# First states on ScalarE's queue, the first half of x in two parts, 23 constant products ahead, and another instruction list: an attention and two-expert-layer kernel on one core

## The chip, the cores and the metric

One core of a Trainium2 chip runs the whole program in one launch. The metric is the device time of one execution in microseconds, lower is better; of several executions the median counts. TensorE (PE) multiplies matrices into PSUM, VectorE (DVE) and ScalarE (ACT) work on tiles in SBUF and PSUM, SyncE (SP) issues transfers. Each engine takes its instructions strictly in the order in which they stand in its own list, and engines wait for each other by semaphores.

## The reference, cut to what matters

```
def _attn_ref(x, state):              # x 4x8x512x64, state 4x8x32x64
    scores = scale * x @ state^T      # softmax over the 32 states -> a
    xread = a @ state
    scores2 = scale * state @ x^T     # softmax over the 512 rows of x -> a2
    sread = a2 @ x
    return concat([xread, sread], axis=2)
def _moe_ref(x, w_in, w_out):         # 2176 tokens, 512 -> 2048 -> 512
    h = x @ w_in
    return (h * tanh(softplus(h))) @ w_out
def _moe2_ref(x, w_gate, w_val, w_out, rms_g):   # 512 -> 1536 -> 512
    xn = x / rms * rms_g
    g = xn @ w_gate
    return (silu(g) * (xn @ w_val)) @ w_out
```

The attention output of four batches (b = 0 to 3) feeds the first layer, and that one feeds the second.

## The kernel before

The kernel records some 2400 operations (`op`), each with its engine, what it reads and writes and a function that issues its instructions. `Plan.run` then goes through a table of numbers, `SEQ`, and issues the operations in exactly that sequence; a number's half is the operation, and an odd number puts an operation that either ScalarE or VectorE can do on VectorE. So `SEQ` alone sets the order in which the instructions stand on each engine and, for the copies that both can do, the engine.

Operands are split into a high and a low float16 part, which costs VectorE and ScalarE much preparation. The first two of four blocks of the first layer for batch 0 (`full_group`) skip the split and use float32 products, so that TensorE has work while the weights are prepared.

What stands at the start, and is touched here:

- `rouse` (L1681) issues 28 products of a constant tile `ones` into an accumulator before anything is loaded. `stir` (L762) issues 40 further products of constants, spread between the first operations of batch 0.
- `load_state` (L631) fetches the states. A batch's 32 states of 8 heads come in two halves, r = 0 and r = 1 (even and odd heads), 32 KB each, on SyncE's queue. For batch 0 a copy of the first half (L393, "COPY attm<-attm") is put behind the second half, so that two transposes give both pairings of heads.
- `attention(0)` (L671) fetches x of batch 0 in two halves of 512 KB (L691), one for even and one for odd heads. TensorE transposes each half in two pieces (L723, four transposes each, into a PSUM bank), which ScalarE or VectorE copies to SBUF (tile `tt`). TensorE transposes the states (L699), VectorE copies them (L393, "COPY attm<-p"), and then the scores of the first half are formed (L754, 16 small products in four accumulators' quarters).
- Of the scores, "s1" is the softmax over states (transposition L793, maxima L807, subtraction L808, exponential L810 on ScalarE, sums and reciprocals L814 to L816, product L819, transposition back L821) and "s2" the one over rows of x (maxima L799 to L802, exponentials L805 on ScalarE).
- Between them VectorE and ScalarE turn the first weights into float32 (L395 and L391 "w<-psm", L501, L508, L512, joined at L528).
- The first real product of the first layer (L999, `l1`) needs the transposed softmax of L821 and the folded weights of L972. Its results go through ScalarE (L1009) to the second product (L1023).
- ScalarE loads a table of functions at the start (L1701), before its first copy.

Of the kernel before, what the change touches and what calls it, by code (L numbers as in the profile page):

```python
# [232 lines left out]
def attn_moe_moe_kernel(  # L233
# [359 lines left out]
    def seven(w, u, m, at, pool, after, store):  # L593
# [33 lines left out]
        for j, n in ((0, 512), (512, 1024), (1536, 1024), (2560, 1024)):  # L627
            split(m, at + j, at + 256 + j + (512 if j else 0), n, s, ((w, u), "s"), f"{w}{u}{j // 512 + 2 if j else 0}")


    def load_state():  # L631
        sv = state.rearrange("b (k r) n d -> b r k n d", r=2)
        for b in range(B):
            for r in range(2):
# [1165 lines left out]
```

## Time and profile before

| what | value |
|---|---|
| runs of the kernel before | 700.97, 701.10, 701.89 us, median 701.1 |
| profiled execution | 702.01 us |
| its span in the trace | 700.2 us |
| TensorE busy | 691.1 us (99%) |
| VectorE busy | 645.3 us (92%) |
| ScalarE busy | 423.1 us (60%) |
| transfers | 101.04 MB, mean 144 GB/s |

The span runs from the first instruction's start to the last one's end; the profiled execution's own time is 1.8 us longer and 0.9 us above the median. In the timeline a row holds the start, the time until the group ends, the engine ("PEld" is TensorE's weight load, "SPq" an issue of a transfer by SyncE), the line, the operation, output and input tiles, shapes, the number of instructions, and in brackets how long the engine had idled and what ended that. Matmuls overlap one another, so a group's pace is read from starts.

### The profile page before, as it was taken

Reading aid. Unit: us, or ns where it says so; the run is one execution under the profiler, and the core shown is the slowest. Engines: PE = TensorE matmul, PEld = TensorE weight load, DVE = VectorE, ACT = ScalarE, POOL = GpSimd, SP = SyncE. Lnnn points to the kernel's source line nnn. Section 1 sums busy time; section 2 is a strip of 40 time slices with the busy share of each in tenths; the row PEclk is TensorE's granted clock in tenths of the full one; section 3 lists DMA queues with packets and bytes.
Section 4 is the critical chain, followed back from the end, with each engine's and each line's share of the span. In section 5 each row is a group of like instructions: output and inputs, shape, how many; then the busy total and the mean of one; then the engine's idle time right before and its main releaser. Section 6 shows DMA issues by size and latency. Waiting matters only on the chain.

```text
span 700.2 us, 14144 instructions
## 1 busy us (share of the span) xinstructions
PE 691.1 (99%) x5834; PEld 491.8 (70%) x5834; DVE 645.3 (92%) x1135; ACT 423.1 (60%) x689; POOL 0.7 (0%) x6
## 2 busy tenths in 40 slices
PE   8999999999999999999999999999999999999997
PEld 6645444444444444476988889988889988899886
DVE  5999999999999999999999998989898897888997
ACT  5999999998877789999947465312212212121330
POOL 0000000000000000000000000000000000000000
PEclk9999999999999999999999999999999999999999
DMA  6977523255255463465800012620455432330233
GB/s 220 284 245 228 182 66 116 65 192 161 81 209 212 168 224 121 150 242 193 334 1 31 31 61 85 232 93 16 136 212 196 152 121 106 135 107 31 91 107 135
DMA packets 42611, 101.04 MB, mean 144 GB/s; under 512 B 16692, under 2 KB 18740, under 8 KB 40116
## 3 DMA queue, kind: packets, MB, share of 16 engines
q1 hardware_dynamic: 42548, 100.15, 41.7%
q8 instruction: 45, 0.74, 0.4%
q14 instruction: 18, 0.15, 0.1%
HBM read 67.90 MB, written 32.24 MB: 143 GB/s over the span
## 4 chain that ended last, share of the span: by engine, by line
PE 56%; DVE 9%; DMA 1%; ACT 1%; issue 1%; SPq 0%; DVEq 0%
PE p L1276 31%; PE a L1360 15%; PE a L1141 4%; PE p L1505 2%; PE p L1073 2%; DMA kept_wg<-attm 1%; DVE g L1103 1%; PE a L1549 1%; DVE attm L625 1%; DVE psm L625 1%; DVE rms L1182 1%; DVE attm L560 1%; DVE rms L955 1%; DVE attm L528 1%; DVE attm L395 1%
## 5 line engine op out<-in xcount | busy, mean ns | idle before, releaser
L1141 PE MATMUL a<-g,w2m 128*128 128x512 f16 (+1 forms) x864 | 162.7, 343 | 0.6 <-DVE slot L1158 0.6
L1141 PEld LDWEIGHTS <-w2m 128*128 128x128 f16 x864 | 75.8, 98 | 79.2 <-issue 4.4
L1276 PEld LDWEIGHTS <-attm 128*128 128x128 f16 x1008 | 98.3, 98 | 13.6 <-issue 2.1
L1276 PEld LDWEIGHTS <-w 128*128 128x128 f16 x1008 | 98.5, 98 | 11.3
L1288 DVE TENSOR_TENSOR tt<-p,tt 128x512 f32<-128x512 f32 x120 | 81.3, 686 | 17.9 <-PE p L1276 16.5
L1065 PE MATMUL p<-slot,rms 128*128 128x512 f16 x336 | 77.3, 379 | 0.3 <-ACT tt L1087 0.3
L1276 PE MATMUL p<-slot,w 128*128 128x256 f16 x576 | 69.3, 273 | 0.0
L1276 PE MATMUL p<-slot,attm 128*128 128x256 f16 x576 | 68.9, 273 | 0.0
L1360 PEld LDWEIGHTS <-w2m 128*128 128x128 f16 x576 | 56.4, 98 | 6.7 <-issue 0.2
L1065 PEld LDWEIGHTS <-rms 128*128 128x128 f16 x336 | 32.2, 98 | 40.9 <-issue 3.4
L1312 ACT ACTIVATE tt<-tt,page 128x512 f32<-128x512 f32 x36 | 25.2, 714 | 54.1 <-DVE tt L1288 54.1
L1360 PE MATMUL a<-attm,w2m 128*128 128x256 f16 x384 | 46.0, 273 | 0.0
L1360 PEld LDWEIGHTS <-g 128*128 128x128 f16 x432 | 42.3, 98 | 4.9
L391 ACT ACTIVATE w2m<-tt 128x512 f16<-128x512 f32 x30 | 18.4, 624 | 43.7 <-DVE tt L1338 21.7
L1087 ACT ACTIVATE tt<-p,page 128x512 f32<-128x512 f32 x60 | 40.3, 680 | 6.6 <-PE p L1065 4.1
L1103 DVE SCALAR_TENSOR_TENSOR g<-tt,page,g 128x1024 f16<-128x1024 f32 (+1 forms) x32 | 38.7, 1211 | 1.3 <-ACT g L391 1.2
L1319 DVE TENSOR_TENSOR w2m<-tt,w2m 128x512 f16<-128x512 f32 x51 | 34.6, 686 | 3.4 <-ACT w2m L391 3.1
L391 ACT ACTIVATE g<-tt 128x512 f16<-128x512 f32 x25 | 15.4, 624 | 36.4 <-DVE tt L1338 28.7
L391 ACT ACTIVATE tt<-p 128x512 f32<-128x512 f32 x31 | 17.9, 592 | 31.8 <-PE p L1276 17.5
L1360 PE MATMUL a<-attm,g 128*128 128x256 f16 x288 | 34.9, 273 | 0.0
L1338 DVE TENSOR_TENSOR tt<-tt 128x512 f32<-128x512 f32 x48 | 32.5, 686 | 0.5
L560 DVE SCALAR_TENSOR_TENSOR psm<-psm,page 128x1024 f16<-128x1024 f32 (+1 forms) x28 | 32.1, 1145 | 0.4 <-ACT psm L391 0.2
(243 smaller groups left out, 1227.4 us busy)
## 6 DMA issues: line engine op xcount, KB each, us to landing
psm<-in_moe_w_out_dram SPq DMA_DIRECT2D x14, 1024.0 KB, 6.3
psm<-in_moe_w_in_dram SPq DMA_DIRECT2D x8, 1024.0 KB, 7.3
psm<-part SPq DMA_DIRECT2D x7, 1024.0 KB, 6.8
psm<-in_moe_w_val_dram SPq DMA_DIRECT2D x6, 1024.0 KB, 5.3
part<-rms SPq DMA_DIRECT2D x24, 256.0 KB, 3.1
kept_wv<-psm SPq DMA_DIRECT2D x9, 512.0 KB
kept_w<-psm SPq DMA_DIRECT2D x9, 512.0 KB, 2.8
attm<-in_moe_w_gate_dram SPq DMA_DIRECT2D x4, 1024.0 KB, 6.2
```

Source lines behind the costliest of these rows:

```text
L391: nc.scalar.activation(o, i, ACTF.Copy, scale=1.0 if scale is None else scale)
L560: op({"V": v1(n) + 0.06}, lambda e: nc.vector.scalar_tensor_tensor(lo, f, s, h, ALU.mult, ALU.subtract), r=[*fn_, *hn, sname], w=ln, name= ...
L1065: nc.tensor.matmul(P[ph], P[folds[u][k]][:, a, f:f + 128], xh[:, k, b, :], start=(k, a, b) == (0, 0, 0), stop=(k, a, b) == (1, 1, 0))
L1087: op({"A": a_ps(512) + 0.1}, lambda e, sp=sp, i=i, ph=ph, ce=ce: nc.scalar.activation(P[sp][:, 512 * i:512 * i + 512], P[ph], ACTF.Mish, s ...
L1103: nc.vector.scalar_tensor_tensor(lo, x, rh, hi, ALU.mult, ALU.subtract)
L1141: nc.tensor.matmul(P[ya[d]][:, :n], part("wo", u, f, a)[:, d * 128:(d + 1) * 128], P[g[0]][:, g[1], b, i * n:(i + 1) * n], start=first and ...
L1276: nc.tensor.matmul(P[to][:, f * 256:f * 256 + 256], part(w, u, j, a)[:, k * 256 + f * 128:k * 256 + f * 128 + 128], h[:, k, b, :], start=b ...
L1288: op({"V": v1(512)}, lambda e: nc.vector.tensor_tensor(P[to], P[bank_], P[a], ALU.add), r=[bank_, a], w=[to], name=f"{w} add")
L1312: op({"A": a_ps(512) + 0.13}, lambda e, i=i, o=o: nc.scalar.activation(P[o], P[i], ACTF.Silu, scale=c3), r=[i, f"c3{u}"], w=[o], tab="silu ...
L1319: op({"V": v1(512)}, lambda e: nc.vector.tensor_tensor(P[g][:, 1, :], P[s], P[g][:, 0, :], ALU.subtract), r=[s], w=[g], name="gl")
L1338: op({"V": v1(512)}, lambda e: nc.vector.tensor_tensor(P[o], P[a], P[b], f), r=[a, b], w=[o], name="gsum")
L1360: nc.tensor.matmul(P[to][:, t * 256:t * 256 + 256], P[g][:, a, o:o + 128], part("w2", u, j, b)[:, f * 256:f * 256 + 256], start=begin and ...
```

## The change

The states of batch 0 are fetched by ScalarE's queue instead of SyncE's. ScalarE's load of the exponential table moves behind the issue of the second half. The first half of x of batch 0 is fetched in two transfers of 256 KB, the second half still in one. `rouse` issues 23 products, not 28. The bookkeeping that holds some buffers back ("hold") issues no instruction and is now one operation ahead of the loads. `SEQ` is replaced by another list of the same length less one entry for "hold" and plus one for the extra load, in which nearly every row differs.

```diff
 SEQ = [int(k) for k in """
-32 46 4 9 58 61 62 0 6 10 50 53 64 74 158 160 48 70 72 66 68 76 116 108 148 114 140 152 118 162 142 126 226 228 230
...
-    def load_state():
+    def load_state(hold):
         sv = state.rearrange("b (k r) n d -> b r k n d", r=2)
         for b in range(B):
             for r in range(2):
-                op({"D": 0.5}, lambda e, b=b, r=r: nc.sync.dma_start(out=sb[:, b, r, :], in_=sv[b, r]),
-                    w=[("state", b, r)], lat=1.9, name=f"state{b} load{r}")
+                def load(e, b=b, r=r):
+                    (nc.sync if b else nc.scalar).dma_start(out=sb[:, b, r, :], in_=sv[b, r])
+                    if (b, r) == (0, 1):
+                        nc.scalar.preload_act_table_set(TABLES["exp"])
+
+                op({"D": 0.5 if b else 0.2}, load, w=[("state", b, r), *([] if b else ["act queue"])], lat=1.9,
+                   after=[] if b else [hold], name=f"state{b} load{r}")
...
-            for r in range(2):
-                a_op({"D": 1.6}, lambda e, r=r: nc.sync.dma_start(
-                    out=P[xb][:, 2 * r:2 * r + 2, :].rearrange("p i (k n) -> p (i k) n", k=2), in_=xv[r]),
-                    r=xbl, w=[(xb, r, 0), (xb, r, 1)], lat=1.9, st=f"load r{r}")
+            for i, n_ in ((0, 1), (1, 1), (2, 2)):
+                k = 2 * i if i < 2 else 0
+                a_op({"D": 0.8 * n_}, lambda e, i=i, n_=n_, k=k: nc.sync.dma_start(
+                    out=P[xb][:, i:i + n_, :].rearrange("p i (k n) -> p (i k) n", k=2), in_=xv[i // 2][:, k:k + 2 * n_, :]),
+                    r=xbl, w=[(xb, i // 2, j) for j in (range(2) if n_ == 2 else [i])], lat=1.9, after=[hold], st=f"load r{i // 2}")
...
-        load_state()
+        load_state(hold)
         load_gain()
         op({"T": 4.0 * ROUSE / 38}, rouse, w=["warm"], name="rouse")
-        nc.scalar.preload_act_table_set(TABLES["exp"])
         state_scale()
-        attention(0)
+        attention(0, hold=hold)
...
-ROUSE, STIRS = 28, 40
+ROUSE, STIRS = 23, 40
```

ScalarE's list at the start of the program, before (p_84 to p_87 are PSUM banks with transposed x, a_88 and a_89 scores of the first half):

```order
L1701 ACT_TABLE_LOAD
L391 ACTIVATE tt<-p_85 128x512
L391 ACTIVATE tt<-p_87 128x512
L391 ACTIVATE tt<-p_84 128x512
L805 ACTIVATE attm,page_103<-a_88,page_69 128x256
```

and in the changed kernel (lines from L631 on are shifted by up to 6; L636 issues a half of the states, L638 loads the table):

```order
L636 DMA attm<-in_state_dram 128x1x64
L391 ACT_TABLE_LOAD
L391 ACTIVATE tt<-p_84 128x512
L636 DMA attm<-in_state_dram 128x1x64
L638 ACT_TABLE_LOAD
L391 ACTIVATE tt<-p_85 128x512
L391 ACTIVATE tt<-p_87 128x512
L391 ACTIVATE tt<-p_84 128x512
L811 ACTIVATE attm,page_102<-a_88,page_69 128x256
```

The first half of the states is ScalarE's first instruction; the second half stands behind ScalarE's first copy of transposed x, and a second table load stands between that and the next copy. VectorE had the first of these copies before.

SyncE's list at the start of the program, before:

```order
L691 DMA attm<-in_x_dram 128x4x256
L635 DMA attm<-in_state_dram 128x1x64 x2
L691 DMA attm<-in_x_dram 128x4x256
L479 DMA psm<-in_moe_w_in_dram 128x4x512 x2
L635 DMA attm<-in_state_dram 128x1x64 x2
```

and in the changed kernel:

```order
L697 DMA attm<-in_x_dram 128x2x256 x2
L697 DMA attm<-in_x_dram 128x4x256
L479 DMA psm<-in_moe_w_in_dram 128x4x512 x2
L636 DMA attm<-in_state_dram 128x1x64 x4
```

The second half of x and the first weights follow x's first half directly; the states of the later batches follow the weights, as before.

VectorE's list from its first copy to the second transposition of scores, before:

```order
L393 COPY attm<-attm 128x64
L393 COPY tt<-p_84 128x512
L393 COPY attm<-p_86 128x256
L793 STREAM_TRANSPOSE attm<-a_88 128x256
L793 STREAM_TRANSPOSE attm<-a_89 128x256
L799 TENSOR_REDUCE page_103<-a_88 128x1
L799 TENSOR_REDUCE page_103<-a_89 128x1
L801 TENSOR_REDUCE page_69<-page_103 128x1
L802 TENSOR_SCALAR page_69<-page_69 128x1
L807 TENSOR_REDUCE page_103<-attm 128x16
```

and in the changed kernel:

```order
L393 COPY attm<-attm 128x64
L393 COPY attm<-p_86 128x256
L805 TENSOR_REDUCE page_102<-a_88 128x1
L805 TENSOR_REDUCE page_102<-a_89 128x1
L807 TENSOR_REDUCE page_69<-page_102 128x1
L808 TENSOR_SCALAR page_69<-page_69 128x1
L799 STREAM_TRANSPOSE attm<-a_88 128x256
L799 STREAM_TRANSPOSE attm<-a_89 128x256
L813 TENSOR_REDUCE page_102<-attm 128x16
```

The maxima of the first half's scores now come ahead of their transposition; from here to the transposition back that the first real product waits for (L821, now L827) VectorE has the same 30 instructions in both kernels.

## Rows read from the trace of the kernel before

**Rows 1.** The page, part 1: busy us, share of the span, instructions

```profile
PE 691.1 (99%) x5834; PEld 491.8 (70%) x5834; DVE 645.3 (92%) x1135; ACT 423.1 (60%) x689; POOL 0.7 (0%) x6
```

**Rows 2.** TensorE's waits, whole span: us in total, times, longest us

```profile
PE a L1141 <- DVE slot L1158: 0.6, 1, 0.6
PE p L1276 <- DVE tt L1288: 0.6, 1, 0.6
...
PE p L1187 <- DVE rms L1182: 0.4, 1, 0.4
...
PE a L1023 <- DVE w2m L528: 0.3, 1, 0.3
PE p L1065 <- ACT tt L1087: 0.3, 1, 0.3
```

**Rows 3.** Stretches: length, busy of PE, PEld, DVE, ACT, POOL, clock, DMA

```profile
50.00:75.00 25.00, 25.00 (x104) 12.16 (x103) 23.98 (x57) 24.77 (x37) 0.00 (x0) 1.00 0.74 237
75.00:100.00 25.00, 25.00 (x194) 11.57 (x192) 24.32 (x46) 24.82 (x39) 0.00 (x0) 1.00 0.41 128
```

**Rows 4.** Timeline, 0 to 22 us

```profile
0.73 1.28 ACT L1701 ACT_TABLE_LOAD   x1 [0.73 <-PEq L1785]
...
0.73 0.44 SPq L691 DMA_DIRECT2D attm<-in_x_dram  x1
...
1.05 5.17 PE L1686 MATMUL a<-ones 128*128 128x256 f16 x28 [1.05 <-DVE ones L1691]
...
1.23 1.36 SPq L635 DMA_DIRECT2D attm<-in_state_dram  x2
...
4.78 0.20 DVE L393 COPY attm<-attm 128x64 f32<-128x64 f32 x1 [3.64 <-DMA attm<-in_state_dram]
...
6.06 1.04 PE L723 MATMUL p<-ident,attm 128*128 128x128 f32 x8
6.69 0.69 DVE L393 COPY tt<-p 128x512 f32<-128x512 f32 x1 [1.71 <-PE p L723]
...
6.82 0.25 PEld L699 LDWEIGHTS p<-ident,attm 128*128 128x128 f32 x2
...
7.13 0.60 ACT L391 ACTIVATE tt<-p 128x512 f32<-128x512 f32 x1 [5.12 <-PE p L723]
...
7.83 0.67 PE L754 MATMUL a<-tt,attm 64*32 64x256 f32 x16 [0.52 <-DVE attm L393]
...
8.58 0.78 DVE L793 STREAM_TRANSPOSE attm<-a 128x256 f32<-128x256 f32 x2 [0.81 <-PE a L754]
...
21.20 0.65 DVE L821 STREAM_TRANSPOSE tt<-attm 128x512 f32<-128x512 f32 x1
...
21.91 0.70 PE L999 MATMUL p<-tt,rms 128*128 128x512 f32 x1 [0.36 <-DVE tt L821]
```

**Rows 5.** TensorE's timeline, two pieces of the constant products

```profile
1.05 4.02 PE L1686 MATMUL a<-ones 128*128 128x256 f16 x18 [1.05 <-DVE ones L1691]
...
4.87 1.24 PE L1686 MATMUL a<-ones 128*128 128x256 f16 x9
```

**Rows 6.** Line L723 within 0 to 10 us: TensorE's own wait for x

```profile
L723 PEldq EVENT_SEMAPHORE  x1: 51/51/51, 4.5 to 4.5; - x1
```

**Rows 7.** The stretch from the first scores on VectorE to L821, columns as rows 3

```profile
8.58:21.20 12.62, 11.45 (x155) 9.45 (x155) 12.24 (x31) 11.52 (x24) 0.00 (x0) 1.00 0.77 259
```

**Rows 8.** The page, part 6: the transfer with the shortest landing, KB, us

```profile
kept_wg<-psm SPq DMA_DIRECT2D x2, 256.0 KB, 2.0
```

**Rows 9.** Tile in_x_dram, 0 to 60 us: from issue to landing

```profile
DMA to landing us min/median/max: 3.2/4.8/5.7
```

**Rows 10.** One stretch while the first weights arrive, columns as rows 3

```profile
9.00:10.00 1.00, 0.52 (x5) 0.28 (x3) 1.00 (x4) 0.88 (x2) 0.00 (x0) 1.00 1.01 377
```

**Rows 11.** The page, part 3: queue, packets, MB, share of 16 engines

```profile
q1 hardware_dynamic: 42548, 100.15, 41.7%
```

More of the change, by code (lines that the diff above doesn't have):

```diff
@@ L669, in states, with attention @@
         return slotm[b](1024, 128, F16).rearrange("p (l n) -> p l n", l=2)
-    def attention(b, due=None):
+    def attention(b, due=None, hold=None):
         a_op = lambda *p, st="", **k: att_ops.append(op(*p, name=f"att{b} {st}", **k))
@@ L1694, in attn_moe_moe_kernel @@
         held = [buf(("held", k), "t") for k in range(6)]
-        hold = op({"X": 0.01}, lambda e: None, w=held, name="hold")
         held2 = [buf(("held", k), "t") for k in range(6, 10)] + [buf(("heldg", k), "g") for k in range(6)]
-        op({"X": 0.01}, lambda e: None, w=held2, after=[hold], name="hold")
-        load_state()
+        hold = op({"X": 0.01}, lambda e: None, w=[*held, *held2], name="hold")
+        load_state(hold)
         load_gain()
         op({"T": 4.0 * ROUSE / 38}, rouse, w=["warm"], name="rouse")
-        nc.scalar.preload_act_table_set(TABLES["exp"])
         state_scale()
-        attention(0)
+        attention(0, hold=hold)
         for u in FULL:
```

197 rows, old and new, of the table SEQ are left out of this document.

## The prediction

> **What bounds the kernel now.** I read the busy times first, then who waits for whom, then the first 22 us instruction by instruction. TensorE is busy 691.1 of 700.2 us [rows 1]; so 9.1 us are all that any new order could win, and most of them lie at the two ends. After the first real product at 21.9 us TensorE's named waits are few: the five of [rows 2] sum to 0.6 + 0.6 + 0.4 + 0.3 + 0.3 = 2.2 us, and four of the five end on VectorE. In the first 100 us VectorE and ScalarE are full as well, 23.98 to 24.82 of 25 us [rows 3]. So there are three nearly full engines, and each is a possible bound: time lost at the start by one of them has little idle time to be made good in. The change works on the start, so the start has to be walked through.
>
> There [rows 4] shows: x is issued at 0.73 us, batch 0's two state halves from 1.23 us. TensorE runs constant products until it transposes the first half of x at 6.06 us, transposes the states at 6.82, and forms scores at 7.83; VectorE begins on the scores at 8.58 us. From there VectorE is busy 12.24 of 12.62 us [rows 7] until L821 at 21.20, and TensorE's first real product waits for that, 0.36 us [rows 4]. So from 8.58 us on VectorE sets the pace: when it gets the first scores decides when real work begins.
>
> **The change part by part.**
>
> *Five constant products fewer.* From 1.05 to 4.87 us 18 products pass, 0.212 us each [rows 5]; from 6.06 to 6.82 us there are seven transposes of half the columns 0.109 us apart [rows 4], and the constants of [rows 5] from 4.87 us on, ten starts to 6.06 us, run at 0.12. The slow pace is that of 256 columns at 1.2 GHz, the fast one at 2.4 GHz. The five taken away are the last, fast ones: 5 x 0.109 = 0.55 us. The transposes can start at 6.06 - 0.55 = 5.51 us. What covers this: x was there by 4.5 us, when TensorE's own wait for it ended [rows 6], and in two parts from the same start it should not be later.
>
> *First states on ScalarE.* The first half is ScalarE's first instruction; nothing precedes it. The second half stands behind ScalarE's copy of the first transposed piece, and that copy waits for TensorE. ScalarE passes its list in order, so the transfer can't be issued at 1.23 us any more: the copy starts as long after the transposes as VectorE's did, 6.69 - 6.06 = 0.63 us [rows 4], so at 5.51 + 0.63 = 6.14 us, and the issue follows the start of the copy, or its end 0.60 us later. How long does it then take? No row shows a transfer on ScalarE's queue. From below the shortest landing is 2.0 us [rows 8]; from above x's longest, 5.7 us [rows 9], behind other transfers in one queue. The first state half needed 4.78 - 1.23 = 3.55 us, behind 512 KB of x. Here the half is small (32 KB) and alone in its queue, but the first weights are streaming at 377 GB/s [rows 10]. I take 2.6 us, nearer to the lower end since nothing is ahead in its queue: it lands at 8.7 us. Ends: 8.1 and 11.9 us.
>
> *What waits for that.* TensorE's next instructions are the state transposes, which need both halves; behind them stand the scores and the transposes of x's second half, so all of TensorE waits. From the state transposes to the scores it was 7.83 - 6.82 = 1.01 us [rows 4]; the scores begin at 8.7 + 1.0 = 9.7 instead of 7.83 us: **+1.9 us**. At the lower end 9.1 us, +1.3; at the upper 12.9 us, +5.1.
>
> *The table load.* A load takes 1.28 us [rows 4]. One now stands between ScalarE's first and second copy: 6.14 + 0.60 + 1.28 + 0.60 = 8.6 us until the second piece is there. That is under 9.1, so the state half hides it; without that cover the scores would still come 0.8 us later than before. The change therefore has no way to bring them earlier. The other load, ahead of the first copy, runs under the constant products.
>
> *x in two parts, x's second half and the weights earlier.* SyncE issues x's second half and the weights ahead of the states, about 1 us sooner. Neither is what the scores wait for, so nothing is gained before 8.58 us; ScalarE's conversion of weights queues behind its exponentials. Zero, hidden behind the scores.
>
> *VectorE's order.* Maxima now come ahead of the transposition, so ScalarE's exponentials come 0.78 us [rows 4] sooner after the scores. But up to L821 VectorE has the same 30 instructions, 12.6 us long [rows 7]; it starts 1.9 us later and ends 1.9 us later. Zero on this path.
>
> *The rest of the list.* Hundreds of rows move, some nine copies go from VectorE to ScalarE. It can win at most the 2.2 us of waits [rows 2], and it can lose as much again or more, since both engines are nearly full early on [rows 3]. The kinds of work ahead of a product look alike in both lists. I take 0, with 2 us either way.
>
> *The sum.* +1.9 us on the profiled execution's 702.0 us (span 700.2 and 1.8 around it) is 703.9; that execution stood 0.9 us above the median. On the median: 701.1 + 1.9 = **703.0 us**. The 0.55 us of constants are not subtracted again: they are inside the 5.51 us.
>
> **The rivals.**
>
> *Absorbed (no change).* The half lands at the lower end, +1.3 us, and VectorE, with fewer copies, makes up a part of it: between +1.3 and -1.3, so 700 to 702.4 us. For it: VectorE waited now and then after 22 us; against it: in [rows 3] it has 0.7 to 1.0 us free per 25 us and ScalarE, which gets the copies, only 0.2.
>
> *Faster.* The mechanism is the moved copies: four of the five waits in [rows 2] end on VectorE. If its list is relieved ahead of just these, up to 1.9 us of them go (0.6 + 0.6 + 0.4 + 0.3). It decides only if the start costs under that: with the landing at its lower end it is 1.3 - 1.9 = -0.6; with one also quicker than any row shows, by the table load's +0.8, -1.1; with ScalarE's wait of 0.3 and an end drawn tighter by 0.6, -2.0, or 699.1 us. It needs all of them.
>
> *Behind the weights.* If the state half is not served between the weights' packets, it lands as late as 11.9 us: +5.1, so 706.2 us. The trace has a single queue [rows 11] and so can't tell how two share the engines. The Trainium skill says, in "DMA: Bandwidth & Descriptors", section "Queues, rings and completion order", that each transfer engine takes turns between queues, a packet at a time. By that rule the half is not held for all the weights, and the sum stays near +1.9; no run here shows it, and I keep the rival at a small chance.
>
> *The clock falls.* TensorE would idle from about 6.4 us, when eight transposes are through, to 8.7. It began at the 1.2 GHz pace after idling and took from 1.05 to 4.87 us of products to leave it [rows 5]. Should it fall back and need as long again, some 4 us of products would run at half pace, 2 us lost: 705.0 us. Against it: an idle of 0.5 us in 9 to 10 us did not lower the clock [rows 10], but 2.3 us is longer than any there.
>
> *It does not do what it says.* That the states come earlier holds for the first half alone; this is the forecast itself.
>
> **How the numbers follow.** Forecast, +1.4 to +3.3 us, 703.0 in the middle: 0.43. Behind the weights, clock, or a list that costs 2 us more on top: 0.18. Absorbed: 0.27. Faster: 0.12. About 0.2%, 1.4 us, is what a measurement of this kernel can tell from no change. So faster 0.12, the same 0.27, slower 0.61. The range: its upper end 706.0 takes in nearly all of the third case but the latest landings; its lower end 700.0 takes in the absorbed case. Outside lie about 0.12 below and 0.07 above. The range of the forecast alone is 702.5 to 704.4 us.
>
> **What would show it.** Right: in the changed kernel ScalarE's issue of the second state half at about 6.1 us or later, TensorE idle before the state transposes for about 2 us until about 8.7, first scores at about 9.7, L827 (the old L821) at about 23.1 us, and the first real product at about 23.8. VectorE's first instruction on scores should follow them by the same 0.75 us. The constant products should end by 5.5 us at 0.109 us each at the end. Wrong: state transposes at 7 us or earlier (the issue didn't wait, or landing takes 1 us); a first real product at 23.8 but an end within 0.5 us of before (the delay is absorbed after the start: then TensorE's waits after 22 us are under 1 us in all); or a start as before and new waits of TensorE between 25 and 350 us (then the list decides, not the start).

## The result, and the profile after

| what | before | after |
|---|---|---|
| median of 6 runs each, on one chip | 702.15 us (700.97 to 702.72) | 709.26 us (708.43 to 710.62) |
| ratio after to before | | 1.0105, 95% interval 1.009 to 1.0119 |
| profiled execution, its span | 702.01, 700.2 us | 710.62, 708.8 us |
| first real product of TensorE | 21.91 us | 29.56 us |

The change costs 7.1 us; 1.9 were forecast, and 709.3 lies above the whole range. The direction and the place were right, the size was not. Below, "the half" is always the second half of batch 0's states.

The page of the changed kernel, busy time and transfer queues (answers to [rows 1] and [rows 11]):

```profile
PE 694.1 (98%) x5829; PEld 492.9 (70%) x5829; DVE 641.9 (91%) x1128; ACT 425.3 (60%) x697; POOL 0.7 (0%) x6
...
q1 hardware_dynamic: 42300, 100.09, 41.3%
...
q10 hardware_dynamic: 264, 0.07, 0.0%
```

The span grew by 8.6 us and TensorE's busy time by 3.0 only: most of the loss is idle time. The queue that is new, q10, is ScalarE's; it carries the two halves and no more. TensorE's timeline of the first 31 us (start, time until the group ends, then as in [rows 4], whose rows these answer):

```profile
1.05 5.09 PE L1692 MATMUL a<-ones 128*128 128x256 f16 x23 [1.05 <-DVE ones L1697]
5.93 1.57 PE L729 MATMUL p<-ident,attm 128*128 128x128 f32 x8
12.90 0.66 PE L705 MATMUL p<-ident,attm 128*128 128x128 f32 x2 [5.39 <-DMA attm<-in_state_dram]
14.16 1.11 PE L760 MATMUL a<-tt,attm 64*32 64x256 f32 x16 [0.61 <-DVE attm L393]
15.20 1.97 PE L729 MATMUL p<-ident,attm 128*128 128x128 f32 x8
...
29.56 1.98 PE L1005 MATMUL p<-tt,rms 128*128 128x512 f32 x4
```

In the kernel before, the same two products of the state transposes (L699; the 6.82 us of [rows 4] is their weight load) stood here:

```profile
6.93 0.38 PE L699 MATMUL p<-ident,attm 128*128 128x128 f32 x2
```

The state transposes (L705 now) start at 12.90 us, 6.0 us later than before, after a wait of 5.39 us for the half. Everything behind them is shifted: scores 14.16 (before 7.83), first real product 29.56 (before 21.91, +7.65). From the first real product to the end it is 708.8 - 29.56 = 679.2 us, before 700.2 - 21.91 = 678.3: the rest hardly changed. ScalarE's timeline of the same stretch shows why the half is late ("ACTq" is an issue of a transfer by ScalarE):

```profile
0.74 1.15 ACTq L636 DMA_DIRECT2D attm<-in_state_dram  x1
1.92 1.28 ACT L391 ACT_TABLE_LOAD   x1 [1.92 <-issue]
7.03 0.60 ACT L391 ACTIVATE tt<-p 128x512 f32<-128x512 f32 x1 [3.83 <-PE p L729]
7.04 0.55 ACTq L636 DMA_DIRECT2D attm<-in_state_dram  x1
7.65 1.28 ACT L638 ACT_TABLE_LOAD   x1
8.94 0.60 ACT L391 ACTIVATE tt<-p 128x512 f32<-128x512 f32 x1
```

The issue stands behind the copy that waits for TensorE, and goes out as that copy starts, at 7.04 us. The chain of work that ended last (start, duration, what) has the other part:

```profile
7.04 5.72 DMA attm<-in_state_dram
```

32 KB took 5.72 us. The busy times by stretch (busy us of each engine with the number of instructions, the granted clock as a share of 2.4 GHz, the share of the transfer engines, GB/s) show what it shared the transfer engines with, and what the wait did to the clock:

```profile
7.00:10.00 3.00, 0.51 (x4) 0.27 (x3) 0.00 (x0) 2.48 (x3) 0.00 (x0) 1.00 1.05 388
10.00:11.00 1.00, 0.00 (x0) 0.00 (x0) 0.00 (x0) 0.00 (x0) 0.00 (x0) 0.72 1.00 367
11.00:12.00 1.00, 0.00 (x0) 0.00 (x0) 0.00 (x0) 0.00 (x0) 0.00 (x0) 0.50 0.73 248
12.00:13.00 1.00, 0.10 (x1) 0.14 (x2) 0.00 (x0) 0.00 (x0) 0.00 (x0) 0.50 0.40 94
13.00:17.00 4.00, 3.39 (x26) 1.97 (x26) 2.01 (x7) 0.60 (x1) 0.00 (x0) 0.50 0.19 43
17.00:18.00 1.00, 0.93 (x13) 0.35 (x16) 0.85 (x2) 0.80 (x2) 0.00 (x0) 0.87 0.00 0
```

The weights stream at 367 to 388 GB/s until about 11 us and run out by 13; the half lands as they run out. TensorE, idle since 7.5 us, is granted 1.2 GHz (0.50) from 10 to 11 us on and gets 2.4 GHz back only after 17 us. So the first products after the wait ran at half pace: the transposes of x's second half (L729 at 15.20) took 1.97 us. In two runs below whose clock stood at 1.00 there (23 constants alone, then both halves first) they took 1.09:

```profile
8.59 1.09 PE L723 MATMUL p<-ident,attm 128*128 128x128 f32 x8
...
9.41 1.09 PE L729 MATMUL p<-ident,attm 128*128 128x128 f32 x8
```

### The profile page after: what moved, and what is told of

It is laid out like the page before. It is cut to its first block, busy times and chain, and to the rows that moved or that the text cites. A ratio compares the mean times of both kernels' runs of the same rounds, so it can differ in the third digit from the quotient of the medians.

```text
span 708.8 us, 14111 instructions
## 1 busy us (share of the span) xinstructions
PE 694.1 (98%) x5829; PEld 492.9 (70%) x5829; DVE 641.9 (91%) x1128; ACT 425.3 (60%) x697; POOL 0.7 (0%) x6
## 4 chain that ended last, share of the span: by engine, by line
PE 68%; DVE 20%; ACT 6%; DMA 3%; issue 2%; DVEq 0%; ACTq 0%
PE p L1282 28%; PE a L1366 15%; PE a L1147 8%; PE p L1071 5%; PE a L1029 4%; PE p L1511 2%; DVE g L1109 1%; DVE psm L560 1%; DVE psm L528 1%; PE a L1555 1%; DMA attm<-in_moe_w_gate_dram 1%; DVE psm L625 1%; PE p L949 1%; PE p L1005 1%; DVE slot L1218 1%
## 5 line engine op out<-in xcount | busy, mean ns | idle before, releaser
L391 ACT ACTIVATE tt<-p 128x512 f32<-128x512 f32 x38 | 22.2, 596 | 71.1 <-PE p L1282 31.3
L1416 DVE SCALAR_TENSOR_TENSOR rms<-a,page,rms 128x512 f32<-128x512 f32 x38 | 28.2, 747 | 8.0 <-issue 4.6
```

What stands on the lines that cost most here:

```text
L391: nc.scalar.activation(o, i, ACTF.Copy, scale=1.0 if scale is None else scale)
L1416: op({"V": v1(512) + 0.06}, lambda e: nc.vector.scalar_tensor_tensor(o(), two(P[bank_]), osc, a(), ALU.mult, ALU.add), r=[bank_, *an, on_] ...
```

## The experiments

Theory A: the half is late because its issue waits behind ScalarE's copy and because, once issued, the transfers in flight on SyncE's queue, the weights above all, keep it from landing; a lower clock adds to it. Rivals: the new list costs the time, or the idle clock does, or ScalarE's queue is slow in itself. Ahead of each measurement stands what was expected. The kernel before had a median of 702.03 us beside the first four runs, 701.92 beside the next four, 701.80 beside the last four; ratios are to these.

### Which queue, and when

**Both halves first on ScalarE's queue.** The changed kernel, with the half's issue moved ahead of ScalarE's first copy:

```diff
-30 0 2 44 58 60 46 62 4 7 8 50 ...
+30 0 2 4 44 58 60 46 62 7 8 50 ...
```

> The changed kernel with one number of its list moved: ScalarE issues the second state half directly behind the first one, ahead of its first copy; the table load moves with it, ahead of the first copy. Theory 1 (the late half is the cause): in the changed kernel it was issued at 7.04 us, landed at 12.87, and the first real product began at 29.56 instead of 21.91 us, +7.65 of +8.6 us of span. Issued at about 1.9 us it lands by about 4.5, the state transposes come at about 7 us, the first real product at 21.5 to 23, and the median at 701.5 to 703.5 us. Theory 2 (the new list is worse after the start, and the start only adds): the start is as early, but the median stays at 705 us or more.

Measured: 703.59 us (701.93 to 704.63), ratio 1.0021 (1.0012 to 1.0031). The loss against the kernel before falls from 7.1 to 1.6 us, just above what theory 1 said. The chain of waits, and TensorE's state transposes, in this kernel:

```profile
1.91 5.75 DMA attm<-in_state_dram
...
7.79 0.42 PE p L705 x2
```

Issued 5 us sooner, the half lands 5 us sooner, but it still takes 5.75 us. Waiting in ScalarE's list was one cause, not the only one. TensorE still waits 1.54 us for the half. Not all of the remaining 1.6 us is this wait: the three executions with a mean granted clock of 0.999 or 1.0 took 701.9 to 703.0 us, the six at 0.996 to 0.998 took 703.1 to 704.6 (the last section shows where the clock fell).

**States on SyncE's queue.** The changed kernel, but batch 0's halves between x's parts on SyncE (x first part, first half, x second part, the half, x's second half, weights), the table load first on ScalarE:

```diff
-                    (nc.sync if b else nc.scalar).dma_start(out=sb[:, b, r, :], in_=sv[b, r])
+                    nc.sync.dma_start(out=sb[:, b, r, :], in_=sv[b, r])
...
```

> The changed kernel with the states of batch 0 back on SyncE's queue, each half directly behind a part of x, and the table load ahead of everything on ScalarE as in the kernel before; list, x in two parts and 23 constant products stay. Theory 1: both halves land by about 5 us, first real product at 21.5 to 23 us, median 701.5 to 703.5 us, as with both halves early on ScalarE's queue. Theory 2 (the list): 705 us or more. What differs from the run with both halves early on ScalarE is the queue alone: within 0.7 us of each other if the queue itself does not matter.

Measured: 701.74 us (700.41 to 703.1), ratio 0.9997 (0.9988 to 1.0007). The new list, x in two parts and 23 constants are still there, and the whole loss is gone. TensorE:

```profile
4.89 1.04 PE L727 MATMUL p<-ident,attm 128*128 128x128 f32 x8
...
5.76 0.38 PE L703 MATMUL p<-ident,attm 128*128 128x128 f32 x2
...
8.82 0.44 PE L727 MATMUL p<-ident,attm 128*128 128x128 f32 x2 [1.40 <-DMA attm<-in_x_dram]
```

The state transposes come at 5.76 us, a microsecond before [rows 4], and win nothing: TensorE then waits for x's second half, 1.40 us.

**One half on each queue.** The changed kernel with the half as SyncE's first transfer and the first half as ScalarE's first instruction: of the change only the half's queue and place are undone. The table load, which stood behind the half's issue, now stands behind the first half's.

```diff
-                    (nc.sync if b else nc.scalar).dma_start(out=sb[:, b, r, :], in_=sv[b, r])
-                    if (b, r) == (0, 1):
+                    (nc.sync if b or r else nc.scalar).dma_start(out=sb[:, b, r, :], in_=sv[b, r])
+                    if (b, r) == (0, 0):
...
```

> The changed kernel with the first state half on ScalarE's queue (its first instruction), the table load behind it, and the second half as the first transfer of SyncE's queue, ahead of x; x in two parts, 23 constants and the new list kept. If a late state half is all that is wrong with the change, both halves land by 4 to 5 us and nothing waits for them: scores at 6.7 to 7.0, first real product at 20.7 to 21.5, 700.3 to 701.5 us, below both kernels. Rival: x's parts are pushed back by the state half and by the shared engines as much as the states gain: 701.7 to 702.

Measured: 702.04 us (700.58 to 704.29), ratio 1.0002 (0.9992 to 1.0011). The whole loss is gone, with list, constants and x's parts kept: the half's queue and place carry it (the table load had ended at 8.93 us in the changed kernel, long before the half landed). The hope of beating both kernels was wrong. TensorE:

```profile
5.74 1.04 PE L729 MATMUL p<-ident,attm 128*128 128x128 f32 x8
6.61 0.38 PE L705 MATMUL p<-ident,attm 128*128 128x128 f32 x2
7.60 0.67 PE L760 MATMUL a<-tt,attm 64*32 64x256 f32 x16 [0.61 <-ACT tt L391]
...
21.81 1.98 PE L1005 MATMUL p<-tt,rms 128*128 128x512 f32 x4
```

Here no transfer is late, the constants last until 5.74, the scores wait 0.61 us for ScalarE's copies of x instead, and the first real product comes at 21.81, as before. From the state transposes to it there are 21.81 - 6.61 = 15.2 us; in the changed kernel 29.56 - 12.90 = 16.7, with the same list. So besides the 6.0 us of lateness the changed kernel loses some 1.5 us behind the wait.

**The kernel before, both halves on ScalarE's queue.** Old list, 28 constants, x in one part; the table load stood ahead of the issues, not behind them as written below.

```diff
-                op({"D": 0.5}, lambda e, b=b, r=r: nc.sync.dma_start(out=sb[:, b, r, :], in_=sv[b, r]),
+                op({"D": 0.5}, lambda e, b=b, r=r: (nc.sync if b else nc.scalar).dma_start(out=sb[:, b, r, :], in_=sv[b, r]),
```

> The kernel before, with batch 0's two state halves issued by ScalarE as its first two instructions, the table load behind them; list, constants and x in one part as before. It asks whether ScalarE's queue costs time though nothing delays its issue. Theory A (a small transfer on another queue is drawn out while SyncE's queue is full): both issued by about 1.8 us, the second lands at 7.5 to 8 us, scores near 8.8, 703.5 to 704 us, as in the run with both halves at once under the new list. Theory B (the 1.85 us between that run and the one with states on SyncE's queue came from the new list's order of weights): states land by 5 to 6 us, 702 us.

Measured: 707.04 us (706.69 to 707.61), ratio 1.0073 (1.006 to 1.0086): worse than either theory said. The chain of waits:

```profile
1.94 8.55 DMA attm<-in_state_dram
...
10.63 0.42 PE p L699 x2
```

Nothing that waits stood ahead of this issue, and the list is the old one: the queue alone costs 5 us, the fall of the clock behind the wait included (granted 0.50 from 12 to 15 us). Theory B, that the new list's order was behind the difference of the first two runs, is out. Against the first run here the half was issued at the same time and landed 2.8 us later; SyncE, with x's first half in one part, issued the weights 0.5 us sooner there (1.77 against 2.25 us). The table load stood ahead of the issues, too. Which of the two decides is not settled.

### What draws the half out

**The half issued at 4.2 us.** The changed kernel with the copy of the first half on ScalarE, ahead of the issue, which so waits for the first half and not for TensorE:

```diff
-30 0 2 44 58 60 46 62 4 7 8 50 ...
+30 0 2 6 4 44 58 60 46 62 8 50 ...
```

> The changed kernel with the second state half issued on ScalarE's queue behind ScalarE's copy of the first state half (VectorE had that copy), which waits for the first half's landing at about 4.0 us. So it is issued at about 4.1 us, after SyncE has issued 2 MB of weights (2.25 to 3.31 us), but three us sooner than in the changed kernel. Theory A (the transfer engines serve what was issued first, whichever queue it came by): its packets move only when the weights are through, at 11 to 12.4 us as in the changed kernel, the state transposes still come at about 12.5 us, and the median stays at 708 to 710 us. Theory B (queues take turns; in the changed kernel the half was late because it was issued late): it lands 2.0 to 3.6 us after the issue, by 6.1 to 7.7 us, the state transposes come at about 7.5 us and the median is 701.5 to 704 us.

Measured: 708.69 us (708.48 to 709.79), ratio 1.0101 (1.0086 to 1.0116). The chain of waits:

```profile
4.22 8.27 DMA attm<-in_state_dram
...
12.62 0.68 PE p L705 x2
```

Issued 2.8 us sooner than in the changed kernel, it landed 0.3 us sooner. In the trace's packets the first of the half's 128 pieces of 256 B moves at 8.7 us, 4.5 us after the issue, and they are strewn thinly up to 11.9 us among 548 of the weights' pieces of 2 KB: the queues do alternate, but the half comes to its end only with the weights.

**The same with the weights later.** Four loads of later batches' states go ahead of the weights on SyncE's queue:

```diff
-30 0 2 6 4 44 58 60 46 62 8 50 53 64 74 160 48 66 ...
+30 0 2 6 4 44 58 60 46 62 8 50 53 64 74 160 48 18 16 10 12 66 ...
```

> As the run with the second half issued at about 4.2 us, and six transfers of the later batches' states put ahead of the first weights on SyncE's queue, so that the weights' packets begin later. Theory A (the weights in flight draw the half out): the half lands earlier than the 12.6 us there, at 6.5 to 9 us, and the scores come that much sooner, 703 to 706 us. Theory B (ScalarE's queue is slow by itself when it is issued to in mid-stream): it lands at 12 us or later again, 708 to 709 us.

Measured: one run, 702.65 us. (Four loads were moved, not six as written there.) The weights' issue moved to 5.02 us. The chain of waits:

```profile
4.14 3.85 DMA attm<-in_state_dram
...
8.13 0.42 PE p L686 x2
```

Same queue, same issue time: 3.85 us instead of 8.27. What stands in SyncE's queue at the time sets the landing. That ScalarE's queue is slow in itself is out.

The transfers of the half side by side, in us (issue and landing from the chains of waits, the pieces from the packets of the traces; "clock held" is the changed kernel with constants in the gap, below):

| kernel | issued | first piece | last piece ends | landed | took | median less before |
|---|---|---|---|---|---|---|
| 4.2 us, weights later | 4.14 | 6.94 | 7.66 | 7.99 | 3.85 | +0.7 (one run) |
| both halves first | 1.91 | 5.42 | 7.25 | 7.66 | 5.75 | +1.6 |
| before, both on ScalarE | 1.94 | 6.32 | 9.87 | 10.49 | 8.55 | +5.1 |
| clock held | 5.75 | 9.64 | 11.98 | 12.33 | 6.58 | +5.9 |
| 4.2 us | 4.22 | 8.67 | 11.95 | 12.49 | 8.27 | +6.7 |
| changed kernel | 7.04 | 11.25 | 12.42 | 12.76 | 5.72 | +7.1 |

In each row half of the time or more passes before the first piece of the half moves: 2.8 us with the weights later, 3.5 to 4.5 us in the others, 2.1 us for the changed kernel's first half, which was issued at 0.74 us, together with x. In the changed kernel it is 4.2 of 5.72 us; then the pieces pass within 1.2 us, as the weights' pieces give out (the last ends at 12.32).

### The clock

**Constants while TensorE waits.** The changed kernel with 46 constant products between x's transposes and the state transposes:

```diff
+            w = ones.bitcast(F16)
+            for _ in range(0 if b else 46):
+                nc.tensor.matmul(P[ps0][:, :256], w[:, :128], w, start=True, stop=True)
```

> The changed kernel with 46 more products of constants (256 columns, 0.109 us each at full clock, 5.0 us) between the transposes of x's first half and those of the states, where TensorE idled from 7.5 to 12.9 us. The half lands as late as before (12.9 us). Theory C (the fallen clock, 0.5 from 10.43 to 17.26 us, cost part of the loss): clock 1.00 throughout after its first rise, the time from the state transposes to the first real product falls from 16.66 to about 15.1 us as in the kernel before, and the median is 1.0 to 1.7 us lower than that of the changed kernel, 707.6 to 708.3 us. If the clock cost nothing: 709.3 us, unchanged. If the constants reach past the landing (they run at half clock): slower than 709.3 us.

Measured: 707.88 us (707.22 to 708.44), ratio 1.0085 (1.0069 to 1.0102): the loss is 5.9 us instead of 7.1. The intervals of the two ratios overlap, so the traces have to carry the reading. TensorE's timeline, and two stretches:

```profile
5.98 5.19 PE L706 MATMUL p<-ones 128*128 128x256 f16 x46
12.46 0.41 PE L708 MATMUL p<-ident,attm 128*128 128x128 f32 x2 [1.30 <-DMA attm<-in_state_dram]
...
28.58 1.98 PE L1008 MATMUL p<-tt,rms 128*128 128x512 f32 x4
```

```profile
10.00:11.00 1.00, 1.00 (x11) 0.79 (x9) 0.00 (x0) 0.00 (x0) 0.00 (x0) 1.00 0.90 339
...
14.00:15.00 1.00, 1.00 (x14) 0.93 (x7) 0.75 (x2) 0.09 (x1) 0.00 (x0) 0.73 0.10 19
```

The granted clock stays at 1.00 through the wait; the state transposes take 0.41 us, not 0.66. It still falls between 14 and 15 us, so the gain is part of what the clock cost and not all of it: from the state transposes to the first real product it is 28.58 - 12.46 = 16.1 us, against 16.7 in the changed kernel and the 15.1 that were expected. Some of the gain is the landing, 0.4 us sooner. Two of the four executions kept a mean granted clock of 1.0; they took 707.2 and 707.7 us.

### The small parts

**23 constants alone**, in the kernel before:

```diff
-ROUSE, STIRS = 28, 40
+ROUSE, STIRS = 23, 40
```

> The kernel before with 23 constant products at the start and nothing else changed: the change's smallest part alone. If the five products taken away are on the path, x's transposes come up to 0.55 us sooner, the states (landing near 6.2 us on SyncE's queue) still in time, scores at 7.3 instead of 7.83 us: 701.5 us. If the states or the clock take the time up again: 702.0, as before. My forecast: 701.7, within 0.1% of before; then the list and the constants of the changed kernel are near zero each, and not a gain and a loss that cancel.

Measured: 701.18 us (700.32 to 702.85), ratio 0.9988 (0.9979 to 0.9997): a gain of 0.7 us (0.2 to 1.5 by the interval), where 0.3 was forecast; five products of 0.109 us would give 0.55.

**18 constants**, in the same place.

> The kernel before with 18 constant products at the start. Even at 1.2 GHz throughout 18 products end at 1.05 + 18 x 0.212 = 4.87 us, so they can't hold x's transposes any more; x's first half was there at 4.5 us. Theory A (the path at the start is constants, then x): with 23 it gained 0.7 us; with 18 the second state half, which landed near 5 us behind x, is next late, so not much more: 700.8 to 701.2 us. Theory B (fewer constants let the clock rise later and cost as much as they give): 702 us, or above.

Measured: 701.18 us (701.03 to 703.12), ratio 0.9994 (0.9985 to 1.0003). No more than 23 gave, and by the interval not clear of no change. TensorE's waits show what is next late:

```profile
6.78 0.41 PE L699 MATMUL p<-ident,attm 128*128 128x128 f32 x2 [0.20 <-DMA attm<-in_state_dram]
```

**States ahead of x, 18 constants.** Both halves as SyncE's first two transfers.

```diff
-32 46 4 9 58 61 62 0 6 10 50 ...
+32 4 6 46 9 58 61 62 0 10 50 ...
...
```

> The kernel before with 18 constant products and both state halves of batch 0 as SyncE's first two transfers, x's first half behind them. One thing differs from the run with 18 constants alone. States land by 3 to 4 us; x's first half, issued about 1.3 us later, by 5 to 5.5 us; transposes of x at 5.1 to 5.5, scores at 6.9 to 7.3 us. If the second state half was the next late thing: 0.3 to 0.8 us faster than 18 constants alone, 700.2 to 700.8. If x, pushed back by the states' issues, is late instead: the same as that run, or 0.5 us slower.

Measured: 702.92 us (701.34 to 704.35), ratio 1.0015 (1.0004 to 1.0026): the rival's direction, and more than its 0.5 us, 1.7 us above 18 constants alone. TensorE now waits for x:

```profile
6.18 1.06 PE L723 MATMUL p<-ident,attm 128*128 128x128 f32 x8 [1.41 <-DMA attm<-in_x_dram]
```

**The new list with x in two parts, 28 constants**, states on SyncE's queue.

> The run with the new list, x in two parts and batch 0's states on SyncE's queue (701.74 us), now with 28 constant products, so that of the change only the list and x's two parts are left. If fewer constants gain 0.7 us here too, as they did under the old list: 702.4 us, and the list with the two parts costs 0.4 us or so against before. If the constants are hidden there: 701.7, and list and parts are worth nothing.

Measured: 701.76 us (700.74 to 702.66), ratio 1.0000 (0.9991 to 1.0009). List and parts together are worth nothing that can be measured; that constants are worth 0.7 us did not show here.

**x in two parts alone**, in the kernel before.

> The kernel before with the first half of x in two transfers of 256 KB and nothing else changed: the last part of the change alone. The second issue on SyncE comes 0.5 us later and pushes the states' issue to 1.7 us. x was waited for in no run; the states land 0.3 to 0.5 us later and still before x's transposes are through (near 5.3 against 6.8 us). So 702.0 us, no change within 0.2%; if x's own landing is what ends the constants' wait, 0.5 us faster, if the states become late, 0.5 us slower.

Measured: 701.75 us (700.94 to 702.91), ratio 0.9999 (0.999 to 1.0008). Nothing, as expected.

## Why the prediction was wrong in size, step by step

- **Five constants fewer: right alone, not in the profiled run.** They were to end at 5.51 us. They ended at 5.93, because all 23 ran at the pace of 1.2 GHz: (5.93 - 1.05) / 23 = 0.212 us each, 256 columns at 1.2 per ns. (The view of stretches prints a granted clock of 1.00 here; the trace's record of the clock begins only with the rise, at 7.02 us.) I took the clock's first rise from one execution [rows 5], as if it were fixed; see the last section.
- **The issue behind ScalarE's copy: right, 0.9 us short.** Forecast 6.14 us, measured 7.04: 0.4 from the constants, the rest because the transposes ran at half pace too (eight in 1.57 us).
- **The landing: the mis-sized term.** I took 2.6 us, "nearer to the lower end since nothing is ahead in its queue"; it took 5.72, the upper end of [rows 9], and 4.2 of that passed before its first piece moved. Being alone in a queue was the wrong row to be near to. The row that counted was [rows 10], 377 GB/s: the transfer engines were full, and the second queue gave the half no way past what was in flight. Of the 4.2 us by which the state transposes missed the forecast, 3.1 are this term. The run with the weights later shows it: 3.85 against 8.27 us.
- **What waits for it: right.** State transposes, scores and VectorE follow in the order given, each by what the half was late.
- **VectorE's chain "zero": 0.9 us too little.** VectorE took 12.6 us from the first scores to the transposition of the softmax [rows 7]; after, from 15.35 to 28.86, 13.5 us. The second scores came late from a TensorE at 1.2 GHz, and VectorE waited 0.65 us for them. With one half on each queue, where the clock did not fall, the same chain took 21.10 - 8.35 = 12.75 us.
- **"x's second half and the weights earlier: zero": wrong, in an indirect way.** Nothing waited for them, but the weights in flight ahead of the half are what kept it from landing (8.27 us, and 3.85 with the weights later). That they went out a microsecond sooner than before is not tested by itself. I costed the transfers that moved by who waits for them, not by whom they hold up.
- **Table load hidden, x in two parts zero, list zero: right.** The load is over at 8.93, long before the half lands; two runs put list with parts at 1.0000 and parts alone at 0.9999, each to 0.1%. (The new list puts seven fewer copies on VectorE, not some nine: it has 1128 instructions instead of 1135.)
- **The rivals "behind the weights" (+5.1) and "the clock falls" (+2): both came, together.** I shared 0.18 between them as if they were alternatives. They are one case: the later the half, the longer TensorE idles. Waits of 3.7, 5.4 and 6.6 us (both on ScalarE in the kernel before, the changed kernel, the half at 4.2 us) came with a fall to 0.50 in the wait or a microsecond behind it, a wait of 1.3 us (clock held) with one two microseconds behind it; with waits of 1.0 and 1.5 us (weights later, both halves first) the clock stood at 1.00 through the wait and up to 20 us. 6.0 us of lateness and the 1.5 us lost behind the wait make 7.5 of the 7.65 by which the first real product is late; the medians differ by 7.1, and the profiled execution was the slowest of its six, 1.4 us above their median.
- **The rule on queues did not help here.** By the Trainium skill, "DMA: Bandwidth & Descriptors", section "Queues, rings and completion order", the transfer engines take turns between queues, a packet at a time, and I read from it that the half would not be held for all the weights. The runs agree that packets of both queues alternate (issued at 4.2 us, the half's are strewn from 8.7 to 11.9 us), but not that the turns are equal or come at once: there 548 pieces of the weights passed between the half's 128, and its first came 4.5 us after the issue. It landed between 12.3 and 12.8 us, near the weights' end, whether it was issued at 4.2, 5.75 or 7.04 us.

What stays open is why the half's first piece comes so late and why it then gets so few turns. In the run with the weights later the transfers beside it were not only other ones but had small pieces (256 B, the weights' 2 KB), and no run here separates the two.

## What to carry to other kernels

A small transfer that is waited for belongs ahead of the big ones in time; here another queue did not protect it while the transfer engines were full, and its landing had to be bounded by the end of the big transfers (12.3 us), not by its own size. An issue placed on a computing engine waits for all that stands ahead of it in that engine's list, so put it before the first instruction that waits. And a start that hangs on three things (constants, x, states) gains little from bringing one of them forward (0.7 us at most here): the next one is late within a microsecond.

## What was not expected of the hardware

- **The same 23 constants took 3.84 to 4.88 us.** From 1.05 us on, the transposes behind them started at 4.89, 5.02, 5.10, 5.22, 5.74 and three times at 5.93 us in eight profiled kernels, in none of them after a wait for data. The step from the 1.2 to the 2.4 GHz pace comes at a different moment each time, under the same instructions: the clock records of these traces begin, with a granted clock of 1.00, between 3.79 and 7.02 us. The start of a profiled execution is uncertain by a microsecond for this alone.
- **The clock fell while TensorE was busy.** In the run with both halves first, TensorE was busy all of 21 to 24 us, and the clock fell there:

```profile
21.00:22.00 1.00, 1.00 (x19) 0.65 (x4) 0.96 (x3) 1.00 (x3) 0.00 (x0) 0.76 0.99 393
22.00:24.00 2.00, 2.00 (x39) 1.67 (x37) 1.97 (x5) 1.59 (x5) 0.00 (x0) 0.50 1.14 318
```

The fall lies between 21 and 22 us. Ahead of it TensorE had been busy 1.64 of the 3 us up to 21, with a wait of 1.09 us for VectorE until 20.76. In the run with one half on each queue it waited 1.08 us at the same place, and the clock stayed at 1.00, so the wait by itself does not decide. The fall is a part of the 1.6 us of the run with both halves first: its executions with the higher mean clock were the faster ones.

- **A 32 KB transfer took 3.85 to 8.55 us** on the same queue, by when it was issued and what another queue had in flight.
